# Attention's weighted sum of the values for two token tiles in one run of products of 256 moving columns, and a new order of the first phase

## The chip, the cores and the metric

The kernel runs on one core of a Trainium2 chip. Its engines work side by side and wait for each other by semaphores: PE (TensorE, matrix products; PEld is its weight load), DVE (VectorE), ACT (ScalarE), POOL (GpSimd), and SP, whose queue issues all the DMAs of this kernel. Matrix products write to PSUM banks; ACT and DVE move the results from there to the on-chip memory, SBUF. The metric is the device time of one execution in microseconds (us).

## The reference

Three layers follow each other on 4608 tokens (8 batches of 576), in float32.

```python
# attention: keys and values are averaged over 8 neighbours, so 72 of each per batch and head
k_p = k.reshape(B, H, Sp, pool, D).mean(axis=3); v_p = v.reshape(B, H, Sp, pool, D).mean(axis=3)
scores = scale * np.matmul(q, k_p.transpose(0, 1, 3, 2))            # 8 heads of 64
attn = softmax(scores); x = np.matmul(attn, v_p)                    # 4608 x 512 when heads are joined
# first layer, w_in 512 x 1024, w_out 1024 x 512
h = x @ w_in; solu = h * softmax(h); ln = (solu - mean) / sqrt(var + 1e-6) * g_ln; y = ln @ w_out
# second layer, w_in 512 x 2048, w_out 2048 x 512
h = y @ w2_in; out = (h * sigmoid(1.702 * h)) @ w2_out
```

## The kernel before

Products of float32 numbers are made of three products of float16 halves: an operand is written as a high half and a low half, and high x high, high x low and low x high are summed in PSUM (`PASSES`).

The work has two phases. The first (up to about 515 us) does attention and the first layer for 36 tiles of 128 tokens and prepares the weights of both layers; it writes y to DRAM. The second does the second layer in 6 blocks of 768 tokens, in a written order (`Up`, `Down`), with products of 384 columns. The change does not touch the second phase.

In the first phase each tile t goes through these steps, named as the profile names them:

- `attention(t)`: DMA `qt`; PE writes the scores to the bank `psx`; DVE takes the row maximum `mx`; the exponential `e` is done by ACT in one instruction after a subtraction on DVE, or by ACT in eight instructions, one for each head (`e<-psx,mx`), whichever queue is shorter by the planner's count; then the sum `rs`, its reciprocal, the division (`e<-e,rs`, mostly on POOL), and the weights as float16 in `st`: high half by ACT (`st<-e`), low half by POOL. A DMA transpose writes `st` to `aT` (16 blocks of 128 x 128). PE then multiplies `aT` with the values `vst`: 16 products with 64 weight columns and 128 moving columns, into the one PSUM bank `psv`. Heads 2p and 2p+1 go to partitions 0 to 63 and 64 to 127 of that bank, so they use the two halves of PE's columns. ACT (`xT<-psv`) and DVE (`xT<-psv,xT`) take the result out as two halves. A tile that lies in two batches (4, 13, 22 and 31) has 32 products of 64 columns instead.
- `hidden`: PE multiplies `xT` with `w1i` in four steps k of six products of 512 columns into `psh` (two buffers); DVE takes the maximum `hmx`, ACT the exponential `he`, DVE the product `tt`, which is the last to read `psh`.
- `norm` and `project`, for two tiles together: ACT and POOL write `zs`, a DMA transpose makes `zT`, and PE multiplies it with `w1o` into `psy` (products of 256 columns, `psy<-zT,w1o`).

Tiles 0 to 3 (`ALONE`) are transposed each by itself; from tile 4 on, the transposes of an even tile wait for those of the odd one and are issued together. `aT` and `xT` have two buffers of one tile each. The bank `psv` has one buffer, and also serves the products `psv<-diag,ones`, which spread a maximum (`v_all`, `w2all`) over all partitions. Beside the tiles run the preparation of keys and values (`half`, `kp`, `vp`, `kbd`, `vx`), of `w_in` and `w_out` of both layers (`raw`, `sgw`, `w1i`, `w1o`, `w_f`, `hi`, `lo`), and the scales for them (`w1i_up`, `w1o_up`).

The order of all instructions of the first phase is set when the kernel is built. Each job is a strand of operations; `Plan.run` takes again and again the operation with the lowest score: its start by a table of costs, shifted by how early or late the strand is against its due time, plus a random number of up to `size`. `DRAWS` gives size and seed of these random numbers by stretches of planned time. Each engine then executes its instructions strictly in that order, and SP issues its DMAs strictly in that order.

Of the kernel before, what the change touches and what calls it, by code (L numbers as in the profile page):

```python
# [9 lines left out]
F32 = mybir.dt.float32  # L10
F16 = mybir.dt.float16
# [3 lines left out]
AF = mybir.ActivationFunctionType  # L15
ALU = mybir.AluOpType
# [4 lines left out]
P = 128  # L21
B, H, S, D = 8, 8, 576, 64
# [56 lines left out]
DNS = 7  # L79
SG = 4  # L80
LAST = 90000
LATE = 3000
LATE_TURN = 3000
TTS = 4
DRAWS = ((70e3, 600, 13), (200e3, 150, 4), (330e3, 150, 13), (1e9, 150, 1))
V_TOP = 2.0 ** 14

TOP3 = 2.0 ** -29 * (1 - 2.0 ** -23)
# [95 lines left out]
class Plan:  # L184
# [31 lines left out]
    def drop(self, *tiles):  # L216
        for t in tiles:
            del self.ring_of[t.name]
# [78 lines left out]
def moe_kernel(ctx: ExitStack, tc: tile.TileContext, qT, kT, vT, w_in, w_out, g_ln, w2_in, w2_out, eye, outT):  # L297
# [138 lines left out]
    with ExitStack() as ph:  # L436
# [25 lines left out]
        def there(*ins):  # L462

            return Op(("none",), lambda engine: None, [], ins, {"none": 0})
# [46 lines left out]
        def V(name, *args, **kw):  # L511
            return op(("dve",), name, args, kw)
# [7 lines left out]
        def A(**kw):  # L520
            return op(("act",), "activation", (), kw)

        def D(dst, src=None, turn=False, short=1):
            pairs = dst if src is None else [(dst, src)]

            def emit(engine):
                for pair in pairs:
                    (nc.sync.dma_start_transpose if turn else nc.sync.dma_start)(*pair)

            outs, ins = ([p[i] for p in pairs] for i in range(2))  # L530
            n = sum(math.prod(x.shape) * mybir.dt.size(x.dtype) for x in outs)
            return Op(("sp",), emit, outs, ins, {"sp": n / 360 * (1.23 if turn else short)}, turn)
# [228 lines left out]
        def spans(t):  # L761

            b0, s0 = divmod(t * P, S)
            n = min(P, S - s0)
            parts = [(0, n, b0)]
            if n < P:
                parts.append((n, P - n, b0 + 1))
            return parts
# [88 lines left out]
        def attention(t):  # L857

            yield lambda: t == 0 or q_loaded[t - 1]
            qt = yield New(sb, [P, NPAIR, P], F32, "qt", bufs=2)  # L860
            q_loaded[t] = True
            yield D(qt, qT[t])
            if t < 2:
                tiles[t].due = max(due(t) + LAG_ATT, DUE_ATT + STEP_ATT * t)
            yield lambda: all(k_ready[b] for _, _, b in spans(t)) and (t == 0 or scored[t - 1])
            e = yield New(sb, [P, H, SP], F32, "e", bufs=2)
            yield there(qt, *(kbd[b % 2] for _, _, b in spans(t)))
            ps = yield New(psx, [P, 2, 512], F32, "psx", "psx")
            yield T(
                [  # L870
                    (
                        ps[o : o + n, p // 2, (p % 2) * 2 * SP : (p % 2 + 1) * 2 * SP],
                        qt[:, p, o : o + n],
                        kbd[b % 2][:, p, :],
                        True,
                        True,
                    )
                    for p in range(NPAIR)
                    for o, n, b in spans(t)
                ]  # L880
            )
            scored[t] = True
            drop(qt)
            s4 = ps[:, :, : 4 * SP].rearrange("p a (h k) -> p a h k", k=SP)
            mx = s1("mx", H)
            m3 = mx.rearrange("p (a h) -> p a h", a=2)
            yield V("tensor_reduce", out=m3, in_=s4, axis=AX.X, op=ALU.max, negate=True)
            if plan.free["act"] + ACT_SPARE < plan.free["dve"]:
                for h in range(H):
                    yield A(out=e[:, h], in_=s4[:, h // 4, h % 4], func=AF.Exp, bias=mx[:, h : h + 1])  # L890
                drop(ps)
            else:
                yield V(
                    "tensor_tensor", out=e.rearrange("p (a h) k -> p a h k", a=2), in0=s4,
                    in1=m3.unsqueeze(3).to_broadcast([P, 2, 4, SP]), op=ALU.add,
                )
                drop(ps)
                yield A(out=e, in_=e, func=AF.Exp)
            rs = s1("rs", H)
            yield V("tensor_reduce", out=rs, in_=e, axis=AX.X, op=ALU.add)  # L900
            yield A(out=rs, in_=rs, func=AF.Copy, scale=1.0 / A_TOP, bias=1e-9 / A_TOP)
            yield V("reciprocal", rs, rs)
            yield VG("tensor_tensor", out=e, in0=e, in1=rs.unsqueeze(2).to_broadcast([P, H, SP]), op=ALU.mult)
            yield lambda: t < 2 or turned[t - 2]
            s = st[t % 2]
            yield A(
                out=s[:, :, 0 : 3 * SP].rearrange("p h (r k) -> p h r k", r=3)[:, :, 0:3:2],
                in_=e.unsqueeze(2).to_broadcast([P, H, 2, SP]), func=AF.Copy,
            )
            yield VG("tensor_tensor", out=s[:, :, SP : 2 * SP], in0=e, in1=s[:, :, 0:SP], op=ALU.subtract)  # L910
            drop(e)
            aT = yield New(sb, [P, 2 * H, P], F16, "aT", bufs=2)
            mine = (aT, s.rearrange("p h c -> p (h c)"))
            if t < ALONE:
                yield D(*mine, turn=True)
                turned[t] = True
            elif t % 2:
                yield lambda: to_turn[t - 1] is not None
                yield D([to_turn[t - 1], mine], turn=True)
                turned[t - 1] = turned[t] = True  # L920
            else:
                to_turn[t] = mine
                yield lambda: turned[t]
            yield lambda: all(v_ready[b] for _, _, b in spans(t)) and (t == 0 or valued[t - 1])
            yield there(aT, *(vst[b % 2] for _, _, b in spans(t)))
            ps = yield New(psv, [P, DM], F32, "psv", "psv")
            yield T(
                [
                    (
                        ps[h % 2 * D64 : (h % 2 + 1) * D64, h // 2 * P + o : h // 2 * P + o + n],  # L930
                        vst[b % 2][:, h // 2 * 2 + c, h % 2 * D64 : (h % 2 + 1) * D64],
                        aT[:, 2 * h + c, o : o + n],
                        c == 0,
                        c == 1,
                    )
                    for p in range(NPAIR)
                    for o, n, b in spans(t)
                    for c in range(2)
                    for h in (2 * p, 2 * p + 1)
                ]  # L940
            )
            valued[t] = True
            drop(aT)
            xT = yield New(sb, [P, 2 * KM, P], F16, "xT", bufs=2)
            turned_x = ps.rearrange("p (k t) -> p k t", t=P)
            yield A(out=xT[:, 0:KM], in_=turned_x, func=AF.Copy, scale=1.0 / A_TOP)
            yield V(
                "scalar_tensor_tensor", out=xT[:, KM:], in0=turned_x, scalar=1.0 / A_TOP, in1=xT[:, 0:KM],
                op0=ALU.mult, op1=ALU.subtract,
            )  # L950
            drop(ps)
            x_turned[t] = xT

        class Pair:

# [6 lines left out]
            def hidden(self, j):  # L962
# [3 lines left out]
                if j == 0:  # L966
                    self.sm, self.mean, self.vs = (s1(n, 2, 4) for n in ("hsm", "mean", "vs"))
                xT = x_turned[t]
                yield there(xT)
                ps = yield New(psh, [P, 2, 512], F32, "psh", "psh", 2)  # L970
                hid[t] = True
                plan.now = due(t)
                for k in range(KM):
                    yield lambda: len(first_done) > 2 * k + 1 and first_done[2 * k].ended and first_done[2 * k + 1].ended
                    yield T(
                        [
                            (
                                ps[:, n, :],
                                xT[:, i * KM + k, :],
                                w1i[w][:, k, n * 512 : (n + 1) * 512],  # L980
                                k == 0 and i == 0 and w == 0,
                                k == KM - 1 and i == 1,
                            )
                            for i, w in PASSES
                            for n in range(2)
                        ]
                    )
                drop(xT)
                yield lambda: all(h_ready[b] for _, _, b in spans(t))
                hp = ps.rearrange("p a c -> p (a c)")  # L990
                s = slice(j, j + 1)
# [278 lines left out]
        k_ready, v_ready, h_ready = ([False] * B for _ in range(3))  # L1270
        q_loaded, scored, turned, valued, hid = ([False] * NTILE for _ in range(5))
        x_turned, to_turn = [None] * NTILE, [None] * NTILE
        first_done, upped = [], set()
        begun = {kind: [0] * B for kind in "kv"}
        yp = tok = None
# [449 lines left out]
```

## Time and profile before

| | us |
|---|---|
| median of 3 runs | 1172.25 (1171.01 to 1172.92) |
| the profiled execution | 1171.01 |
| its span, first to last instruction | 1169.0 |
| PE busy in the span | 1125.7 (96%) |
| ACT busy | 754.7 (65%) |
| DVE busy | 724.4 (62%) |
| POOL busy | 617.7 (53%) |

Busy time of PE counts every moment in which a product is under way, also where it waits for its weights; so a stretch of PE at 9 tenths is not one in which nothing can be won. The view by stretches tells where engines are idle, the view of the waits tells for whom, and the view of instructions in order of time tells when.

### The profile page before, as it was taken

To read this page: it belongs to the slowest core of one execution; us is meant where nothing else is said; L and a number is where in the kernel's file an instruction comes from. 1 tells how busy PE (TensorE), PEld (TensorE's weight loads), DVE (VectorE), ACT (ScalarE), POOL (GpSimd) and SP (SyncE) were. 2 spreads that over 40 slices of the span, in tenths; PEclk is the share of its full clock that TensorE was granted. 3 is DMA by queue.
4 is the path that set the end of the run, shared out by engine and by line. 5 is a ranking of instruction groups with operands and counts; after the bars stand their busy time and mean duration, and the time that the engine had idled before them with its cause. 6 is when DMAs were issued, how large, how long until landed. Compare 5 with 4: busy or idle time off the path is not lost.

```text
span 1169.0 us, 19696 instructions
## 1 busy us (share of the span) xinstructions
PE 1125.7 (96%) x7737; PEld 726.1 (62%) x7737; DVE 724.4 (62%) x1105; ACT 754.7 (65%) x997; POOL 617.7 (53%) x643
## 2 busy tenths in 40 slices
PE   4888999999999999999999999999999999999998
PEld 4555676667676667765566656666666665566655
DVE  7988888777677753426753773567266636753650
ACT  6889998989798874737624752674367337625740
POOL 4566999989999985315503530561056016403530
PEclk9989999999999999999999999999999999999999
DMA  9979999999999768355465355536453653463131
GB/s 356 277 191 278 243 280 282 278 275 273 270 244 226 178 172 262 85 195 193 146 200 174 125 176 163 180 127 202 142 174 126 214 178 127 149 202 117 60 121 60
DMA packets 247356, 225.75 MB, mean 193 GB/s; under 512 B 165728, under 2 KB 218080, under 8 KB 246752
## 3 DMA queue, kind: packets, MB, share of 16 engines
q1 hardware_dynamic: 247264, 224.50, 67.0%
q8 instruction: 60, 0.98, 0.3%
q14 instruction: 32, 0.26, 0.1%
HBM read 151.06 MB, written 33.55 MB: 158 GB/s over the span
## 4 chain that ended last, share of the span: by engine, by line
PE 69%; POOL 13%; ACT 6%; DVE 5%; DMA 5%; issue 2%; SPq 1%; POOLq 0%; ACTq 0%; DVEq 0%
PE bank_a L1385 31%; PE bank_d L1385 16%; PE bank_b L1385 8%; PE psy L537 6%; PE psh L537 5%; POOL w_f L496 3%; PE psv L537 2%; POOL lo L496 2%; POOL zs L496 2%; POOL st L496 1%; POOL e L496 1%; PE psx L537 1%; DMA w2i_dram<-lo 1%; POOL q L496 1%; DMA raw<-w_out 1%
## 5 line engine op out<-in xcount | busy, mean ns | idle before, releaser
L1385 PEld LDWEIGHTS <-w2o 128*128 128x128 f16 x2016 | 197.0, 98 | 130.4
L1385 PEld LDWEIGHTS <-w2i 128*128 128x128 f16 x1974 | 193.1, 98 | 129.9 <-issue 2.4
L349 POOL TENSOR_TENSOR w_g<-w_g 128x384 f32<-128x384 f32 x42 | 46.1, 1097 | 399.2 <-ACT w_g L1464 399.2
L1479 DVE SCALAR_TENSOR_TENSOR g<-w_g,gu_b,g 128x1152 f16<-128x1152 f32 (+1 forms) x96 | 175.4, 1828 | 92.0 <-ACT g L1474 91.7
L1385 PE MATMUL bank_a<-ys,w2i 128*128 128x384 f16 x1128 | 205.6, 326 | 0.9 <-ACT c L1404 0.9
L537 PE MATMUL psh<-w1i,xT 128*128 128x512 f16 x864 | 201.8, 384 | 3.5 <-ACT xT L496 3.1
L1385 PE MATMUL bank_a<-g,w2o 128*128 128x384 f16 x1152 | 201.6, 326 | 0.0
L537 PEld LDWEIGHTS <-w1o 128*128 128x128 f16 x1728 | 168.0, 98 | 30.8 <-DMA zT<-zs 2.8
L537 PE MATMUL psy<-zT,w1o 128*128 128x256 f16 x1536 | 176.2, 273 | 3.5 <-DMA zT<-zs 2.3
L1474 ACT ACTIVATE g<-w_g,gu_b 128x1152 f16<-128x1152 f32 (+1 forms) x96 | 134.3, 1411 | 50.3 <-POOL w_g L352 39.3
L1404 ACT ACTIVATE c<-bank_a 128x384 f32<-128x384 f32 x188 | 90.7, 483 | 102.4 <-PE bank_a L1385 101.8
L537 PEld LDWEIGHTS <-xT 128*128 128x128 f16 x864 | 83.4, 99 | 96.3 <-issue 6.0
L1385 PE MATMUL bank_d<-g,w2o 128*128 128x384 f16 x576 | 104.2, 326 | 0.0
L496 POOL TENSOR_TENSOR zs<-tt,zs 128x1024 f16<-128x1024 f32 x36 | 78.4, 2178 | 44.2 <-ACT zs L496 43.8
L1385 PE MATMUL bank_d<-ys,w2i 128*128 128x384 f16 x564 | 101.1, 326 | 0.0
L1464 ACT ACTIVATE w_g<-c,ch_b 128x1536 f32<-128x1536 f32 x47 | 73.8, 1570 | 28.7 <-DVE c L1407 28.7
L352 POOL TENSOR_TENSOR w_g<-w_g 128x384 f32<-128x384 f32 x42 | 83.2, 1982 | 0.0
L1407 DVE SCALAR_TENSOR_TENSOR c<-bank_d,c 128x384 f32<-128x384 f32 x94 | 51.9, 552 | 41.9 <-ACT c L1404 29.6
L496 POOL TENSOR_TENSOR lo<-w_f,hi 128x512 f16<-128x512 f32 (+1 forms) x48 | 65.8, 1389 | 6.6 <-ACT e L496 2.9
L496 DVE TENSOR_REDUCE hmx<-psh 128x1 f32<-128x1024 f32 x36 | 43.8, 1218 | 36.2 <-PE psh L537 36.2
L537 PE MATMUL psx<-kbd,qt 128*128 128x144 f32 (+1 forms) x320 | 47.8, 312 | 15.1 <-ACT kbd L496 9.6
L496 DVE CUSTOM_DVE_ANT_0 tt<-psh,he 128x1024 f32<-128x1024 f32 x36 | 43.8, 1218 | 23.1 <-ACT he L496 22.9
(205 smaller groups left out, 1606.8 us busy)
## 6 DMA issues: line engine op xcount, KB each, us to landing
w2i<-w2i_dram SPq DMA_DIRECT2D x48, 896.0 KB, 4.6
w2o<-w2o_dram SPq DMA_DIRECT2D x84, 512.0 KB, 3.7
half<-kT SPq DMA_DIRECT2D x16, 576.0 KB, 6.4
half<-vT SPq DMA_DIRECT2D x16, 576.0 KB, 6.2
qt<-qT SPq DMA_DIRECT2D x36, 256.0 KB, 4.7
y_dram<-y SPq DMA_DIRECT2D x36, 256.0 KB, 3.5
y<-y_dram SPq DMA_DIRECT2D x48, 192.0 KB, 4.0
raw<-w_in SPq DMA_DIRECT2D x16, 512.0 KB, 7.7
```

The source lines that it names most:

```text
L349: eng.tensor_tensor(out=w[:, 1], in0=q[:, Q12], in1=q[:, Q11], op=ALU.subtract)
L352: eng.tensor_tensor(out=w[:, 3], in0=q[:, Q21], in1=w[:, 2], op=ALU.subtract)
L496: getattr(eng, name)(*args, **kw)
L537: nc.tensor.matmul(*p[:3], start=p[3], stop=p[4], skip_group_check=len(p) > 5)
L1385: nc.tensor.matmul(bank, self.weight(p, kk, w), self.data(p, kk, i), start=(first and kk == 0 and w == 0 and i == 0), stop=(last and kk == ...
L1404: nc.scalar.activation(out=self.c[:, i], in_=getattr(self, bank), func=AF.Copy, scale=self.scale)
L1407: nc.vector.scalar_tensor_tensor(out=self.c[:, i], in0=getattr(self, bank), scalar=self.scale, in1=self.c[:, i], op0=ALU.mult, op1=ALU.add,)
L1464: nc.scalar.activation(out=self.w[:, 0:4], in_=self.c, func=AF.Gelu_apprx_sigmoid, scale=self.ch)
L1474: nc.scalar.activation(out=self.g[s.start][:, 0], in_=self.w[:, s], func=AF.Copy, scale=self.gu)
L1479: nc.vector.scalar_tensor_tensor(out=self.g[s.start][:, 1], in0=self.w[:, s], scalar=self.gu, in1=self.g[s.start][:, 0], op0=ALU.mult, op1 ...
```

## The change

`attention` of an even tile from 4 on ends after its weights are made, and leaves its transpose to the odd tile. A new function `weigh` does the products for one tile (tiles 0 to 3) or for a pair. For a pair `aT` holds both tiles side by side (256 columns), and the products run in two rounds, each with half of the heads: 8 products of 256 columns into `psv`, then out by ACT and DVE, then the other round into the same bank. Where the pair lies in two batches, each weight block has two products whose columns add up to 256. `aT` and `xT` are twice as wide and keep two buffers, so they hold four tiles in place of two. A `hidden` product may begin when two of its four k steps are there (`KM_FIRST`).

```diff
-DRAWS = ((70e3, 600, 13), (200e3, 150, 4), (330e3, 150, 13), (1e9, 150, 1))
+DRAWS = ((70000.0, 600, 12), (80000.0, 150, 12), (200000.0, 150, 118705), (450000.0, 150, 372612), (1000000000.0, 150, 263081))
...
-            aT = yield New(sb, [P, 2 * H, P], F16, "aT", bufs=2)
-            mine = (aT, s.rearrange("p h c -> p (h c)"))
+            if t < ALONE or t % 2 == 0:
+                aT = yield New(sb, [P, 2 * H, 2, P], F16, "aT", bufs=2)
+                mine = (aT[:, :, 0], s.rearrange("p h c -> p (h c)"))
...
+                yield D([other, (aT[:, :, 1], s.rearrange("p h c -> p (h c)"))], turn=True)
...
+            yield from weigh([t] if t < ALONE else [t - 1, t], aT)
+        def weigh(ts, aT):
...
+            wide, rounds = len(ts) * P, len(ts)
+            kr = KM // rounds
+            yield lambda: all(v_ready[b] for _, _, b in parts) and (ts[0] == 0 or valued[ts[0] - 1])
+            yield there(aT, *(vst[b % 2] for _, _, b in parts))
+            xT = yield New(sb, [P, 2, KM, 2 * P], F16, "xT", bufs=2)
+            flat = aT.rearrange("p c j t -> p c (j t)")
+            for r in range(rounds):
+                ps = yield New(psv, [P, DM], F32, "psv", "psv")
+                yield T(
...
+                            flat[:, 2 * h + c, o : o + n],
...
+                yield A(out=xT[:, 0, ks, :wide], in_=turned_x, func=AF.Copy, scale=1.0 / A_TOP)
...
+                drop(ps)
```

The new order shows at three places. The first is ACT at the start, from the first keys (`kbd`) on; `sgw` and `raw` are conversions of `w_in`, `e` and `st` belong to tile 0. Before:

```order
L496 ACTIVATE kbd_133<-kp 64x4x72 x2
L496 ACTIVATE sgw<-raw_z 128x1024
L496 ACTIVATE raw_z<-raw_z 128x1024 x2
L496 ACTIVATE e<-e 128x576
L496 ACTIVATE sgw<-raw_z 128x1024
L496 ACTIVATE raw_z<-raw_z 128x1024 x2
L496 ACTIVATE rs<-rs 128x8
L496 ACTIVATE diag_253<-eye_t,vam 128x128
L496 ACTIVATE st_135<-e 128x8x2x72
```

And now, the last twelve of the twenty rows from `kbd` on that stand ahead of the first `st`:

```order
L497 ACTIVATE raw_z<-raw_z 128x1024
L497 ACTIVATE e<-psx,mx 128x72 x2
L497 ACTIVATE sgw<-raw 128x1024
L497 ACTIVATE e<-psx,mx 128x72 x2
L497 ACTIVATE raw<-raw 128x1024
L497 ACTIVATE e<-psx,mx 128x72
L497 ACTIVATE vx<-vp,v_up 128x4x144
L497 ACTIVATE e<-psx,mx 128x72
L497 ACTIVATE raw<-raw 128x1024
L497 ACTIVATE rs<-rs 128x8
L497 ACTIVATE sgw<-raw 128x1024
L497 ACTIVATE raw<-raw 128x1024
```

Tile 0's exponential is now in eight instructions, and three more `raw`, two more `sgw` and `vx` stand ahead of the first `st`.

The second place is DVE between the conversions of `w_out` and the second tile's `tt` (`ISA tt`). Before:

```order
L496 SCALAR_TENSOR_TENSOR raw<-raw 128x1024
L496 TENSOR_TENSOR e<-psx,mx 128x576
L496 SCALAR_TENSOR_TENSOR xT<-psv,xT 128x512
L496 TENSOR_SCALAR nm<-hmx,h_sc 128x1
L496 SCALAR_TENSOR_TENSOR raw<-raw 128x1024
L496 TENSOR_REDUCE hmx<-psh 128x1
L496 TENSOR_REDUCE rs<-e 128x8
L496 TENSOR_REDUCE mx<-psx 128x8
L496 RECIPROCAL rs<-rs 128x8
L496 TENSOR_SCALAR nm<-hmx,h_sc 128x1
L496 TENSOR_TENSOR e<-psx,mx 128x576
L496 ISA tt,mean<-psh,he 128x1024
```

And now, with the second tile's own `hmx` at the top:

```order
L497 TENSOR_REDUCE hmx<-psh 128x1
L497 TENSOR_SCALAR galln<-galln 128x1
L497 TENSOR_SCALAR nm<-hmx,h_sc 128x1
L497 TENSOR_SCALAR pw_g<-galln 128x1
L497 RECIPROCAL rc_g<-pw_g 128x1
L497 TENSOR_REDUCE mx<-psx 128x8
L497 TENSOR_SCALAR g_up<-rc_g 128x1
L497 TENSOR_SCALAR g_dn<-pw_g 128x1
L497 TENSOR_TENSOR e<-psx,mx 128x576
L497 SCALAR_TENSOR_TENSOR xT<-psv,xT 128x4x128
L497 TENSOR_SCALAR g_col<-g_col,g_up 128x8
L497 ISA tt,mean<-psh,he 128x1024
```

The third tile's `hmx` and the conversions `raw` of `w_out` no longer stand between the second tile's `hmx` and its `tt`.

The third place is PE between the two rounds of the second pair (tiles 6 and 7). Before, between the last product of tile 6 and the first of tile 7:

```order
L537 LDWEIGHTS vst_132
L537 MATMUL psv<-aT,vst_132 64x128
L537 MATMUL psx<-kbd_133,qt 128x144 x4
L537 LDWEIGHTS vst_132
L537 MATMUL psv<-aT,vst_132 64x128
```

And now, between the two rounds of that pair:

```order
L538 LDWEIGHTS vst_132
L538 MATMUL psv<-aT,vst_132 64x256
L538 MATMUL psx<-kbd_133,qt 128x144 x4
L538 LDWEIGHTS vst_132
L538 MATMUL psv<-aT,vst_132 64x256
```

The same four score products stand between the two uses of the bank. Over the whole first phase PE has 416 products of `aT` in place of 640.

## Rows read from the trace of the kernel before

**Rows 1.** Busy time by stretches: stretch, PE, PEld, DVE, ACT, POOL, clock, DMA, GB/s.
```profile
0.00:87.00 87.00, 60.56 (x405) 44.40 (x406) 73.26 (x139) 68.06 (x96) 46.83 (x55) 0.94 0.93 274
117.00:515.00 398.00, 388.52 (x3143) 274.70 (x3142) 263.32 (x475) 316.83 (x459) 326.27 (x391) 1.00 0.92 230
```

**Rows 2.** Instructions in order of time on PE: start, length, columns, idle before.
```profile
431.26 2.78 PE L537 MATMUL psy<-zT,w1o 128*128 128x256 f16 x24
433.88 4.05 PE L537 MATMUL psh<-w1i,xT 128*128 128x512 f16 x18
437.86 0.64 PE L537 MATMUL psv<-aT,vst 128*64 128x128 f16 x16
438.43 2.79 PE L537 MATMUL psy<-zT,w1o 128*128 128x256 f16 x24
...
84.47 0.69 PE L537 MATMUL psv<-aT,vst 128*64 128x64 f16 x32
85.09 1.25 PE L537 MATMUL psx<-kbd,qt 128*128 128x144 f32 x8
```

**Rows 3.** PE's waits: for whom, us in total, times, longest.
```profile
PE psv L537 <- DVE xT L496: 4.6, 6, 1.7
PE psv L537 <- DVE w2all L496: 2.2, 1, 2.2
```

**Rows 4.** Instructions of the tile psv: count, least, median and longest ns.
```profile
L496 ACT ACTIVATE xT<-psv x36: 571/586/618, 35.4 to 453.7; 128x512 f16<-128x512 f32 x36
L496 DVE SCALAR_TENSOR_TENSOR xT<-psv,xT x36: 678/689/693, 36.7 to 454.8; 128x512 f16<-128x512 f32 x36
```

**Rows 5.** PE in order of time around the second tile's end.
```profile
69.07 0.22 PE L537 MATMUL psy<-diag,ones 128*128 128x128 bf16 x1 [2.41 <-ACT kp L496]
71.40 0.27 PE L537 MATMUL psy<-diag,ones 128*128 128x128 bf16 x1 [2.11 <-DVE mean L496]
71.46 2.77 PE L537 MATMUL psh<-w1i,xT 128*128 128x512 f16 x6
74.02 2.13 PE L537 MATMUL psx<-kbd,qt 128*128 128x144 f32 x8
```

**Rows 6.** Busy time by stretches, the same place.
```profile
70.40:77.20 6.80, 5.80 (x18) 3.44 (x18) 4.47 (x23) 4.04 (x8) 5.40 (x13) 0.50 0.87 174
74.00:76.00 2.00, 2.00 (x10) 1.89 (x9) 0.00 (x0) 0.69 (x2) 1.92 (x4) 0.50 0.75 81
```

**Rows 7.** DVE and ACT in order of time, the same place.
```profile
60.22 1.21 DVE L496 TENSOR_REDUCE hmx<-psh 128x1 f32<-128x1024 f32 x1
69.92 1.22 DVE L496 CUSTOM_DVE_ANT_0 tt<-psh,he 128x1024 f32<-128x1024 f32 x1
...
67.91 0.21 ACT L496 ACTIVATION_READ_ACCUMULATOR he<-psh,nm,h_sc 128x1 f32 x1
```

**Rows 8.** ACT in order of time, and the tile e: the start of the kernel.
```profile
12.21 2.13 ACT L496 ACTIVATE raw_z<-raw_z 128x1024 uint32<-128x1024 uint32 x2
20.28 1.17 ACT L496 ACTIVATE st<-e 128x1152 f16<-128x1152 f32 x1 [1.17 <-POOL e L496]
...
L496 ACT ACTIVATE e<-e x35: 666/672/705, 14.2 to 414.1; 128x576 f32<-128x576 f32 x35
L496 ACT ACTIVATE e<-psx,mx x8: 303/330/366, 381.0 to 394.2; 128x72 f32<-128x72 f32 x8
```

**Rows 9.** PE in order of time: the first weighted sum and the first hidden product.
```profile
31.12 0.64 PE L537 MATMUL psv<-aT,vst 128*64 128x128 f16 x16 [0.66 <-DMA vst<-vx]
36.06 2.59 PE L537 MATMUL psh<-w1i,xT 128*128 128x512 f16 x6 [3.12 <-ACT xT L496]
```

**Rows 10.** DMA issues (count, median us to landing), and a wait of SP's queue.
```profile
aT<-st SPq DMA_TRANSPOSE x36, 5.0
zT<-zs SPq DMA_TRANSPOSE x36, 4.0
...
SPq L528 <- PE psv L537: 10.2, 5, 4.7
```

More of the change, by code (lines that the diff above doesn't have):

```diff
@@ L81 @@
 LAST = 90000
+KM_FIRST = 2
 LATE = 3000
@@ L918, in attention @@
                 yield lambda: to_turn[t - 1] is not None
-                yield D([to_turn[t - 1], mine], turn=True)
+                aT, other = to_turn[t - 1]
+                yield D([other, (aT[:, :, 1], s.rearrange("p h c -> p (h c)"))], turn=True)
                 turned[t - 1] = turned[t] = True
             else:
[L922 to L952, printed above, removed]
+                to_turn[t] = aT, mine
@@ new lines, in attention @@
+                return
+            yield from weigh([t] if t < ALONE else [t - 1, t], aT)
+        def weigh(ts, aT):
+            parts = []
+            for j, t in enumerate(ts):
+                for o, n, b in spans(t):
+                    if parts and parts[-1][2] == b:
+                        parts[-1][1] += n
+                    else:
+                        parts.append([j * P + o, n, b])
+            wide, rounds = len(ts) * P, len(ts)
[7 more added lines that the diff above has]
+                yield T(
+                    [
+                        (
+                            ps[h % 2 * D64 : (h % 2 + 1) * D64, (h // 2 - r * kr) * wide + o : (h // 2 - r * kr) * wide + o + n],
+                            vst[b % 2][:, h // 2 * 2 + c, h % 2 * D64 : (h % 2 + 1) * D64],
+                            flat[:, 2 * h + c, o : o + n],
+                            c == 0,
+                            c == 1,
+                        )
+                        for p in range(r * kr, (r + 1) * kr)
+                        for o, n, b in parts
+                        for c in range(2)
+                        for h in (2 * p, 2 * p + 1)
+                    ]
+                )
+                if r == rounds - 1:
+                    for t in ts:
+                        valued[t] = True
+                    drop(aT)
+                ks = slice(r * kr, (r + 1) * kr)
+                turned_x = ps.rearrange("p (k t) -> p k t", t=wide)
+                yield A(out=xT[:, 0, ks, :wide], in_=turned_x, func=AF.Copy, scale=1.0 / A_TOP)
+                yield V(
+                    "scalar_tensor_tensor", out=xT[:, 1, ks, :wide], in0=turned_x, scalar=1.0 / A_TOP,
+                    in1=xT[:, 0, ks, :wide], op0=ALU.mult, op1=ALU.subtract,
+                )
+                drop(ps)
+                for t in ts:
+                    x_parts[t] += kr
+                    x_turned[t] = xT
+            x_left[xT.name] = len(ts)
@@ L968, in hidden @@
                 xT = x_turned[t]
-                yield there(xT)
+                mine = slice(0 if t < ALONE else t % 2 * P, P if t < ALONE else (t % 2 + 1) * P)
+                yield lambda: x_parts[t] >= KM_FIRST or x_parts[t] == KM
+                yield there(xT[:, :, : x_parts[t], mine])
                 ps = yield New(psh, [P, 2, 512], F32, "psh", "psh", 2)
@@ L973, in hidden @@
                 for k in range(KM):
+                    yield lambda: x_parts[t] > k
                     yield lambda: len(first_done) > 2 * k + 1 and first_done[2 * k].ended and first_done[2 * k + 1].ended
@@ L978, in hidden @@
                                 ps[:, n, :],
-                                xT[:, i * KM + k, :],
+                                xT[:, i, k, mine],
                                 w1i[w][:, k, n * 512 : (n + 1) * 512],
@@ L987, in hidden @@
                     )
-                drop(xT)
+                yield lambda: xT.name in x_left
+                x_left[xT.name] -= 1
+                if not x_left[xT.name]:
+                    drop(xT)
                 yield lambda: all(h_ready[b] for _, _, b in spans(t))
@@ L1272, in moe_kernel @@
         x_turned, to_turn = [None] * NTILE, [None] * NTILE
+        x_parts, x_left = [0] * NTILE, {}
         first_done, upped = [], set()
```

## The prediction

> **What bounds the kernel now.** I read the busy time by stretches first. From 117 to 515 us, the bulk of the first phase, PE is busy 388.5 of 398 us, and no other engine over 326 [rows 1]; in the first 87 us it is busy 60.6 of 87, with DVE (73.3) and ACT (68.1) both busier than PE. So the first phase has two regimes: a start in which DVE and ACT set the pace, and a long part in which PE does. Second I read PE in order of time, to see what a weighted sum costs there: 16 products of 128 columns start at 437.86 and the next work at 438.43, so 0.57 us [rows 2]. Third, PE's waits: the bank `psv` is waited for in most of those after the start, 4.6 us in six waits for the eviction of an earlier tile and 2.2 us in one for a maximum [rows 3]. Last, the costliest single place on PE, around 70 us, from three views: two waits of 2.41 and 2.11 us, then products at half speed [rows 5, 6]. The second phase is untouched, and begins when the first ends.
>
> All sums are made against the profiled execution: 1171.01 us, of which 1169.0 are the span and 2.0 lie around it. The median shown is 1172.25, 1.24 more; I add the sum to the median, as another kernel's median would carry the same surplus.
>
> **The product itself: 0.** Before, a pair of tiles has two groups of 16 products, 2 x 0.57 = 1.14 us on PE. What are the 0.57? A product of 256 columns on the whole array takes 2.62 / 24 = 0.109 us (431.26 to 433.88), so 128 columns take 0.055; 16 of them one after another would be 0.87. Only 0.57 pass, so the two heads of a pair run side by side, in 8 x 0.055 = 0.44 us, and 0.13 us are entry and exit. Now a pair of tiles has two rounds of 8 products of 256 columns: 4 side-by-side pairs x 0.109 = 0.44, plus entry and exit 0.13: again 0.57 a round. The number of columns and of groups is the same; what goes is half of the weight loads, and these lie beside the products. Bounds: if entry and exit vanished, 32 rounds x 0.13 = 4.2 us are won. If wide products did not run side by side, a round is 8 x 0.109 + 0.13 = 1.0, and 32 x 0.43 = 13.8 us are lost; nothing but the width speaks for that. I take 0, since the 64-column form fits too: 32 products in 0.62 us [rows 2] is shorter than 16 x 0.055, so pairs overlap at either width. The pairs with two batches change as little: tile 4 and tile 5 cost 0.62 + 0.57, and now two rounds of eight narrow and eight 192-column products.
>
> The Trainium skill has a rule that would give more: TensorE: Matmul & The Clock Gate, section "Back-to-back issue gap", says that in a stream of weight loads and products the spacing is set by both, some 81 ns at 128 columns and 131 ns at 512. By it halving the loads would pay; but here 16 loads and products of 128 columns pass in 0.57 us, 36 ns each, so the trace does not show loads that set the pace.
>
> **Evictions: 0.** ACT and DVE still take 512 columns out of `psv` 36 times, at 0.59 and 0.69 us [rows 4]: 32 for pairs, 4 for the first tiles.
>
> **The bank psv: +0.4.** Both rounds use the one bank, so the second waits until ACT and DVE have emptied it, about 1.3 us plus the way between the engines, and more when their queues hold other work. In PE's order I counted how often at most 2.6 us of PE work (by the rates of rows 2) stand between one use of the bank and a following weighted sum: 18 times before, 19 times now. Of these, follow-ups of one weighted sum on another are 8 before and 12 now; sums behind a maximum are 10 and 7. The waits seen are 6.8 us over 18 places, 0.38 each, so +0.4. Bounds: all gone, -6.8; each of the four added short follow-ups at the longest wait seen, 1.7: +6.8.
>
> **The early stall: -4.** At 66.7 to 71.5 PE stands for 2.41 + 2.11 us, and then runs at half clock until 77.2 (0.50 granted, the 1.2 GHz level): six products of 512 columns take 2.56 us from 71.46 to 74.02, where 18 took 3.98 at 433.88, so 1.33 for six. That is 1.2 lost, and as much again in the next 3 us: 6.9 in all. The next hidden product could not start before, since both `psh` buffers were full until the second tile's `tt` ended at 71.1; and `tt` came 8.5 us after its own `hmx` had ended, behind the third tile's `hmx` and two conversions, though ACT's `he` had ended at 68.1 [rows 7]. In the new order DVE has only small scalings, one `mx`, one subtraction and one `xT` between the two, so `tt` waits for `he`, and `psh` comes free some 2 to 4 us earlier. PE's order helps too: 30 products of `psh` now stand before the product for `w1o` that waited. But the whole 6.9 cannot be won: DVE is the busier engine here, and idle for only about 2.3 us of it, 74.0 to 76.0 in full [rows 6]. I take 4, between 2.3 (DVE's idle time) and 6.9; if the stall forms anew elsewhere, 0.
>
> **The start: +1.** Tile 0's exponential is now eight instructions on ACT, 8 x 0.33 = 2.6 us in place of one of 0.67, and three `raw` and two `sgw` (1.07 each, [rows 8]) and `vx` (an estimate of 0.6, half of an `st` for half of its columns) go first: 2.0 + 5.3 + 0.6 = 7.9 us, less 1.2 in which ACT was idle. So the first `st` ends some 6 us later than 21.45, and the first weighted sum, at 31.12 before, comes at about 37, the first hidden product at 38 to 39 in place of 36.06 [rows 9]. Behind a late `st` there is nothing on ACT that was not going to be done: the conversions that overtake it are the ones the hidden product needs for its weights. So PE gets most of it back when the four steps of that product run without a break. Bounds: -1 (they are ready together) to +6 (all of it stays).
>
> **The wider buffers: 0.** SP's queue waited five times for a weighted sum to free `aT`, 10.2 us in all [rows 10]; with four tiles of room that goes. No wait of PE for `aT` is in the view of the waits, so nothing shows on PE. Bound: the bank's 4.6 us, if evictions came earlier through it.
>
> A rule of the Trainium skill speaks against the change here. DMA: Bandwidth & Descriptors, section "Latency and other measured facts", says that a DMA transpose whose middle dimension is not contiguous moves some 30% less. The target of `aT` becomes that (blocks of one tile lie 256 columns apart). But `zT` has that form already, with the same size, and lands in 4.0 us at the median against 5.0 for today's `aT` [rows 10]; the trace does not agree, and the sum takes nothing for it.
>
> **Sum.** 0 + 0.4 - 4 + 1 + 0 = -2.6 us, and -1 more for the half clock behind the one long bank wait (2.2 us, [rows 3]) if, as likely as not, that meeting does not recur: half of 2.2. So -3.6: 1167.4 against the profiled execution, 1168.7 for the median.
>
> **Rivals.**
> - More is won: the early stall goes in full (-6.9), and so do most bank waits (-4 of 6.8), since tiles are finished further ahead in wider buffers. For it: these are all waits on work that was only queued late. Against: ACT and DVE are at 80% and 66% even in PE's part, so queues stay. 1172.25 - 10.9, about 1161.5.
> - It does not do what it says: the stall of 70 us is DVE's pace, not its order, and moves to the next place. DVE is busy 73.3 of the first 87 us, the work is the same, and every other term is near nothing: 1172.
> - Slower: the late first tile decides. DVE sits in its queue behind tile 0's sum `rs`, which needs all eight exponentials; what follows it there (the last maxima of `w_in`, and so the scale of `w1i`) is late too, and a regime paced by DVE never gets it back. It decides if more than the 4 us of the early stall stay: +6 from the start, 0 from the stall less a bank wait or two, about +4: 1176.
> - Wide products do not run side by side, or transposes to the split target are slow enough to be waited for: +13.8 for the first, 1186.
>
> **How the numbers follow.** Forecast (1166 to 1171) 0.36; more is won 0.21; no change 0.22; slower from the start 0.16; wide products or transposes 0.05. The likeliest is 1168.7. A measurement of this kernel tells 0.2%, 2.3 us, from no change. Faster by more than that: 0.34 of the forecast's and all of the second, 0.55. Slower: 0.16 + 0.05 = 0.21. Within: the rest, 0.24. The range that holds 8 in 10 reaches from 1160.5 (a part of the second beyond it) to 1175.5 (half of the slower case inside).
>
> **What would show it.** In the new profile a round of eight wide products should be followed by PE's next work after 0.55 to 0.60 us; under 0.5, or at 1.0, that step is wrong. The first weighted sum should stand near 37 us and the first hidden product near 39. Around 65 to 77 us there should be no two waits of over 2 us in a row and no half clock; if there are, elsewhere before 117 us, the second rival holds. Waits for `psv` should sum to 6 to 8 us. The stretch from 515 us on, shifted, should be the same. What would make the prediction wrong above all is a start whose delay is passed on by DVE, or an order whose queues meet better than I can see from counts.

## The result, and the profile after

The changed kernel takes 1184.69 us (median of 6, 1180.32 to 1188.49), the kernel before 1172.65 beside it. The ratio is 1.0095, 95% interval 1.0077 to 1.0113: slower, where I had said 1168.7 and faster. The profiled execution took 1188.49 us, its span 1186.7; before it was 1171.01 and 1169.0. From span to span 17.7 us are lost, between the medians 12.0: the profiled execution is the slowest of the changed kernel's six, that of the kernel before the fastest of its six, so some 6 of the 17.7 us belong to these two executions and not to the change. PE's busy time grew by 3.9 (1125.7 to 1129.6), its idle time by 13.8 (43.3 to 57.1).

Where? Busy time of the changed kernel by stretches, columns as in [rows 1]:

```profile
0.00:87.00 87.00, 56.72 (x389) 42.09 (x390) 70.69 (x135) 68.06 (x103) 47.98 (x54) 0.97 0.84 267
117.00:200.00 83.00, 74.74 (x555) 50.72 (x553) 64.78 (x111) 67.36 (x98) 69.52 (x78) 0.94 1.11 256
117.00:531.00 414.00, 394.24 (x2942) 273.93 (x2940) 271.18 (x482) 315.84 (x457) 318.88 (x387) 0.98 0.91 222
```

and of the kernel before, the stretch that [rows 1] does not show apart:

```profile
117.00:200.00 83.00, 81.30 (x665) 57.21 (x664) 68.39 (x117) 73.63 (x107) 79.69 (x91) 1.00 1.05 270
```

The first phase now ends near 531 us, not 515. Between 117 us and its end PE is idle for 19.8 us (414 less 394.2) where it was for 9.5. From 117 to 200 us every engine does less than before (PE 74.74 for 81.30, GpSimd 69.52 for 79.69), and PE's clock is 0.94 of full in place of 1.00.

PE's waits in the changed kernel, as [rows 3]:

```profile
PE psv L538 <- DVE xT L497: 13.4, 5, 5.5
PE psv L538 <- DMA aT<-st: 9.2, 6, 3.4
PE psv L538 <- DVE w2all L497: 1.2, 1, 1.2
```

The eviction of an earlier weighted sum is waited for 13.4 us, before 4.6. The wait of a weighted sum for its transposes, 9.2 us, had no line before. The longest of both from 60 to 200 us, on PE in order of time:

```profile
89.17 1.06 PE L538 MATMUL psv<-aT,vst 128*64 128x64 f16 x16 [5.50 <-DVE xT L497]
...
125.26 0.30 PE L538 MATMUL psv<-aT,vst 128*64 128x128 f16 x4 [2.57 <-DMA aT<-st]
127.14 0.85 PE L538 MATMUL psv<-aT,vst 128*64 128x128 f16 x12 [1.57 <-DMA aT<-st]
...
168.57 1.07 PE L538 MATMUL psv<-aT,vst 128*64 128x192 f16 x16 [3.44 <-DMA aT<-st]
```

Around each the granted clock is at the 1.2 GHz level, here at the second and the third:

```profile
126.80:130.20 3.40, 3.06 (x18) 1.51 (x18) 1.05 (x2) 2.17 (x3) 3.40 (x3) 0.50 1.01 315
167.80:174.60 6.80, 6.03 (x28) 2.60 (x28) 2.96 (x5) 2.49 (x4) 6.80 (x7) 0.50 0.86 259
```

In the first phase of this execution 30.6 us are spent at that clock, before 13.6, which is more than enough for the 3.9 us of added busy time: six products of `psh` are listed with 2.59 us at 127.92, at half clock, and with 1.46 at 121.23. In large part it is the execution's own: its mean granted clock is 0.987 of full, some 31 us at half clock, and that of the other five 0.990 to 0.992, 19 to 24 us.

What I had promised of the product itself is there. One round of eight wide products, on PE:

```profile
153.80 0.63 PE L538 MATMUL psv<-aT,vst 128*64 128x256 f16 x8
154.35 1.25 PE L538 MATMUL psx<-kbd,qt 128*128 128x144 f32 x8
```

0.55 us to the next work, against 0.57 for the group of 16 in [rows 2].

### The profile page after: what moved, and what is told of

Its sections match the earlier page's. It is cut to its first block, busy times and chain, and to the rows that moved or that the text cites. A ratio compares the mean times of both kernels' runs of the same rounds, so it can differ in the third digit from the quotient of the medians.

```text
span 1186.7 us, 19252 instructions
## 1 busy us (share of the span) xinstructions
PE 1129.6 (95%) x7513; PEld 724.3 (61%) x7513; DVE 731.4 (62%) x1108; ACT 753.9 (64%) x1004; POOL 611.2 (52%) x639
## 4 chain that ended last, share of the span: by engine, by line
PE 69%; POOL 10%; ACT 6%; DMA 5%; DVE 5%; issue 3%; SPq 1%; POOLq 0%; ACTq 0%; DVEq 0%
PE bank_a L1416 31%; PE bank_d L1416 15%; PE bank_b L1416 8%; PE psy L538 7%; PE psh L538 6%; PE psv L538 3%; POOL lo L497 2%; POOL w_f L497 2%; POOL e L497 1%; POOL st L497 1%; DVE raw L497 1%; DMA w2i_dram<-lo 1%; DMA aT<-st 1%; DMA raw<-w_in 1%; PE psx L538 1%
## 5 line engine op out<-in xcount | busy, mean ns | idle before, releaser
L497 POOL TENSOR_TENSOR lo<-w_f,hi 128x512 f16<-128x512 f32 (+1 forms) x44 | 60.7, 1393 | 6.4 <-ACT hi L497 2.7
L538 PE MATMUL psx<-kbd,qt 128*128 128x144 f32 (+1 forms) x320 | 44.6, 299 | 18.7 <-DMA qt<-qT 10.8
L538 PEld LDWEIGHTS psx<-kbd,qt 128*128 128x128 f32 (+1 forms) x320 | 40.0, 186 | 29.5 <-issue 15.4
```

Source lines behind the costliest of these rows:

```text
L497: getattr(eng, name)(*args, **kw)
L538: nc.tensor.matmul(*p[:3], start=p[3], stop=p[4], skip_group_check=len(p) > 5)
```

## The experiments

Theory O: the pairing is worth next to nothing, and the new order of the first phase costs. Theory P: the pairing itself costs, since a pair needs both transposes before it can begin, and uses the one bank twice in a row.

### Other draws for both structures

Only the table of random numbers is changed: the kernel before with the table of the changed one, and the reverse; then both without random numbers.

```diff
-DRAWS = ((70e3, 600, 13), (200e3, 150, 4), (330e3, 150, 13), (1e9, 150, 1))
+DRAWS = ((70000.0, 600, 12), (80000.0, 150, 12), (200000.0, 150, 118705), ...)   # e1, on before
+DRAWS = ((1e9, 0, 1),)                                                           # e3, on before
```

The second and fourth run make the like edits of the changed kernel.

> The kernel before, unchanged but for its random numbers: it gets the sizes and seeds that the changed kernel has. Theory O (the loss comes from the order that happens to be drawn, not from pairing): this one is slower than before too, by some 5 to 18 us (1177 to 1190). Theory P (pairing itself costs, since a pair's product needs both transposes and the one bank twice): about as before, 1169 to 1176.

> The changed kernel with the random numbers of the kernel before. Theory O: a draw like any other, anywhere from 1173 to 1195, on no side of the changed kernel's 1184.7 for a reason. Theory P: 1182 to 1190.

> The kernel before with random numbers of size zero: the planner's own order. Theory O: slower than before by 5 to 20 us. Theory P: within 4 us of before.

> The changed kernel with random numbers of size zero. Theory O: within 6 us of e3_before_no_draws on either side. Theory P: some 12 us above it.

Measured: 1187.15 (ratio 1.0126, 1.0109 to 1.0143), 1190.98 (1.0161, 1.0145 to 1.0178), 1184.40 (1.0096, 1.0071 to 1.0121) and 1180.72 (1.0071, 1.0052 to 1.0090). Every other order is slower than the kernel before, also with the products of one tile. Without random numbers the pair's kernel has the lower median of the two, though the intervals overlap. The kernel before with the other table has the changed kernel's waits, though it pairs nothing:

```profile
PE psv L537 <- DVE xT L496: 13.1, 6, 5.8
PE psv L537 <- DMA aT<-st: 7.9, 3, 3.4
```

That is for O, but not clean: a table does not give the same order to two structures.

### The orders exchanged

So I wrote the orders down, operation by operation, and let each structure run in the other's. A pair's first half stands where the even tile's product and eviction stood, its second half where the odd one's stood; nothing else moves. One line has to move for it, so that the second buffer of `xT` is not asked for before the first is free:

```diff
-            xT = yield New(sb, [P, 2, KM, 2 * P], F16, "xT", bufs=2)
             for r in range(rounds):
                 ps = yield New(psv, [P, DM], F32, "psv", "psv")
                 yield T(...)
+                if r == 0:
+                    xT = yield New(sb, [P, 2, KM, 2 * P], F16, "xT", bufs=2)
```

The reverse run takes the functions of the kernel before, with `aT` and `xT` at `bufs=4`, and the changed kernel's order.

> The changed kernel's pairs, but every engine works in the order of the kernel before: the product of a pair's first half stands where the even tile's product stood, that of its second half where the odd tile's stood, and the evictions likewise (xT is allotted behind the first product, so that nothing else is moved). Theory O (the order is what costs): within 0.3% of the before of this call, about 1170 to 1176 us, and the longest waits of the changed kernel (5.5 us for an eviction at 89 us, 3 to 4 us for transposes at 125 and 168 us) are gone. Theory P (the pairing itself costs): about 1183 us or more, since both transposes and the bank still have to come first.

> The reverse: the kernel before's products, one tile at a time and 128 columns wide, each evicted by itself, but every engine works in the order of the changed kernel (the even tile's product stands where the pair's first half stood; aT and xT get four buffers of a tile each, the same memory as two of a pair). Theory O: as slow as the changed kernel, 1181 to 1188 us, with PE's waits for aT of 5 to 10 us in all at the same places (125 to 127 and 168 us) and the eviction's wait at 89 us. Theory P: near the before of this call, about 1173 us.

Measured: pairs in the old order 1168.87 (1167.96 to 1170.46; ratio 0.9963, 0.9950 to 0.9977), a little below what theory O said; single tiles in the new order 1183.64 (1180.31 to 1186.05; 1.0087, 1.0070 to 1.0103). The time goes with the order and not with the pairing. Nor is it the half clock: the single tiles' profiled execution was granted 0.997 of the full clock, some 7 us at half clock, and took 1184.30 us. PE's waits, first of the pairs in the old order, where no line names `aT`:

```profile
PE psv L636 <- DVE xT L595: 5.9, 9, 1.7
```

then of the single tiles in the new order:

```profile
PE psv L639 <- DVE xT L598: 11.8, 5, 5.8
PE psv L639 <- DMA aT<-st: 7.1, 3, 2.6
```

Why the old order does not wait shows on SP's queue (a line is the time in which it issues) beside PE's. Pairs in the old order:

```profile
108.58 6.96 SPq L627 DMA_TRANSPOSE zT<-zs  x2
115.63 3.90 SPq L627 DMA_TRANSPOSE aT<-st  x2
...
132.42 0.64 PE L636 MATMUL psv<-aT,vst 128*64 128x128 f16 x16
```

The changed kernel:

```profile
111.57 9.52 SPq L529 DMA_TRANSPOSE zT<-zs  x2
121.18 3.77 SPq L529 DMA_TRANSPOSE aT<-st  x2
...
121.23 1.46 PE L538 MATMUL psh<-w1i,xT 128*128 128x512 f16 x6
```

In the old order the transposes of tiles 8 and 9 have been issued at 119.5 and their weighted sum starts at 132.42, with 12.9 us of room. In the new order they have been issued at 124.95, and PE, which came to the product at 122.69, starts it at 125.26 and stops in it again until 127.14. PE comes to the product 9.7 us sooner than in the old order, and SP to the end of the transposes 5.4 us later.

Pairs in the old order are faster than both kernels. That 0.37% (0.23 to 0.50) is the worth there of the pairing with its wider buffers, 4.3 us. One profile of each does not show where it lies: the spans are 1168.7 and 1169.0, though the medians are 4 apart.

### One more draw

> The kernel before, products of one tile, with the same four stretches and sizes of the draw but the seeds 100 to 103 in place of 13, 4, 13 and 1. Theory O: a drawn order of the kernel before is worth about as much as any other, 1178 to 1192 us, so that 1173 us is the lucky end. Theory P: within 0.4% of the kernel before.

1192.47 (1.0165, 1.0146 to 1.0184). This is just above theory O's range. With the two above, three other orders of the kernel before cost 11 to 19 us; how the table of its own order was chosen, no run shows. PE from 117 to 200 us in this one:

```profile
117.00:200.00 83.00, 72.58 (x543) 49.47 (x542) 60.08 (x120) 66.86 (x97) 66.24 (x79) 0.96 1.06 262
```

A slow order need not wait for the transposes: PE waits 1.6 us for `aT` here, and in the kernel before without random numbers 1.5:

```profile
PE psv L537 <- DMA aT<-st: 1.5, 1, 1.5
```

### Can the waits be moved away?

Three places of the changed kernel's order, by hand; all else stays. The list names operations of the order and is not code.

```diff
 ACT:  w1o, w1o, w1o, w1o,
-      w1o, w1o, zs, w1o, w1o, tt, xT (tiles 4 and 5, first half), st, zs, e, xT (second half)
+      xT (first half), w1o, w1o, zs, w1o, xT (second half), w1o, tt, st, zs, e
 PE:
-      psv (tiles 8 and 9, first half), psh, psx (tile 12), psv (second half), psh, psh, psh, psx (tile 13), psy
+      psh, psx (tile 12), psh, psh, psv (first half), psh, psx (tile 13), psy, psv (second half)
       (tiles 12 and 13 likewise behind three pieces of psh)
```

> The changed kernel in its own order but for three places. Tiles 4 and 5: the first half's eviction on ACT goes ahead of four w1o conversions, and the second half's product ahead of the psx of tile 8. Tiles 8 and 9: the first half's product goes behind three more pieces of psh, the second half's behind them. Tiles 12 and 13: the first half's goes behind three pieces of psh, the second behind a piece of psy and of psh. Theory O: the waits of 5.5, 4.1 and 3.4 us go, and with them up to three stretches at half clock (1.7 us lost in each 3.4 us of it), so 8 to 18 us less than the changed kernel: 1167 to 1177 us. Theory P: the transposes are late for what follows too, and less than 5 us comes back: 1180 us or more.

1187.36 (1.0116, 1.0099 to 1.0133): nothing came back, where theory O, for which the exchange had spoken, had 1167 to 1177. By stretches, this kernel:

```profile
60.00:90.00 30.00, 26.80 (x194) 17.34 (x193) 25.41 (x56) 25.91 (x39) 17.04 (x20) 1.00 0.57 155
90.00:117.00 27.00, 19.68 (x134) 12.72 (x133) 22.96 (x46) 24.04 (x38) 18.03 (x28) 1.00 1.11 268
```

and the changed kernel:

```profile
60.00:90.00 30.00, 22.95 (x174) 15.81 (x172) 25.46 (x55) 25.97 (x39) 17.23 (x20) 0.93 0.60 169
90.00:117.00 27.00, 26.56 (x170) 16.34 (x167) 24.75 (x55) 25.64 (x42) 18.91 (x31) 0.95 1.11 265
```

PE wins 3.9 us up to 90 us and loses 6.9 up to 117. ACT and DVE do the same work in the first stretch as they did (25.9 and 25.4 of 30), so PE only came sooner to what they had not yet made. The operations tell the same: the hidden products behind tiles 4 and 5 start at 85.81 us in place of 90.17, the products of `w1o` behind them at 117.86 in place of 115.99. At the second place PE waited for a load instead:

```profile
131.27 2.26 PE L636 MATMUL psx<-kbd,qt 128*128 128x144 f32 x8 [5.42 <-DMA qt<-qT]
```

That `qt` stood in SP's queue behind the same transposes. So a second try leaves the place of tiles 4 and 5 alone, and puts the loads of `qt` for tiles 12 and 13 ahead of the transposes:

```diff
-SP: zT (pair 1) x2, aT (tiles 8 and 9) x2, y_dram, qt (12), qt (13)
+SP: qt (12), zT (pair 1) x2, qt (13), aT (tiles 8 and 9) x2, y_dram
```

> The changed kernel in its own order but for two places: the products of tiles 8 and 9 and of tiles 12 and 13 moved behind later pieces of psh, as in the run with three places, and SP's load of qt for tile 12 put ahead of the zT transposes, that for tile 13 ahead of the aT transposes, so that the psx of tile 12 does not wait for it (5.42 us there). The eviction of tiles 4 and 5 stays where the changed kernel has it. If single waits of PE are the price of this order (local), 4.1 and 3.4 us of waits and some 5 us of half clock go: 1171 to 1177 us. If the engines that feed PE are late there as well (given back), PE waits at the next place instead and the time stays at 1181 to 1188 us.

1180.74 (1178.99 to 1185.88; 1.0080, 1.0054 to 1.0105), some 4 us under the changed kernel, but the intervals overlap. From 117 to 200 us:

```profile
117.00:200.00 83.00, 74.74 (x575) 51.08 (x573) 66.06 (x118) 71.08 (x105) 73.04 (x81) 1.00 1.09 267
```

PE is busy for 74.74 us, as in the changed kernel, but the clock is back at 1.00 and it gets further: the product of a maximum that the changed kernel starts at 188.04 starts 5.3 us sooner (this profiled execution is the fastest of its six). First the changed kernel, then this one:

```profile
188.04 0.22 PE L538 MATMUL psv<-diag,ones 128*128 128x128 bf16 x1
182.76 0.22 PE L636 MATMUL psv<-diag,ones 128*128 128x128 bf16 x1
```

The waits for `aT` fell from 9.2 to 3.1, and others stand in their place:

```profile
139.30 2.75 PE L636 MATMUL psh<-w1i,xT 128*128 128x512 f16 x12 [1.54 <-DVE mean L595]
143.45 0.22 PE L636 MATMUL psv<-diag,ones 128*128 128x128 bf16 x1 [1.40 <-ACT diag L595]
...
176.23 5.40 PE L636 MATMUL psy<-zT,w1o 128*128 128x256 f16 x48 [1.77 <-ACT y L595]
```

Single waits as the whole price would have won 8 to 14 us (1171 to 1177); the medians lie 4 apart, and 1180.74 is 0.3 below the range for an outcome in which all is given back. So a few microseconds may be local, and the larger part is given back at the next places.

### Is one feeding engine short?

Two edits of both kernels, each in its own order. The first narrows the low parts of `w2` on GpSimd and stores the high ones in their place; the second leaves the stores of the low parts out.

```diff
-yield VG("tensor_tensor", out=lo[:, s], in0=w[:, s], in1=hi[:, s], op=ALU.subtract)
+yield VG("tensor_tensor", out=lo[:, s, :32], in0=w[:, s, :32], in1=hi[:, s, :32], op=ALU.subtract)   # e9, e10
...
-yield D(self.dst[1], lo)
+yield D(self.dst[1], hi)                       # e9, e10
+(no store; the second phase reads hi twice)    # e11, e12
```

> The changed kernel in its own order, with less work for GpSimd: the subtraction that makes the low parts of w2 (lo<-w_f,hi, 48 of them, 1.16 us and 2.6 us each) covers 32 of 256 columns, and the high part is stored a second time in place of the low part, so the low parts of w2 are wrong and the bytes moved are the same. Some 55 us of GpSimd's work between 127 and 440 us go. Theory G (the new order starves GpSimd, which before worked 79.7 of the 83 us from 117 to 200): most of the 11.5 us comes back, and the distance to the same edit of the kernel before is under 5 us. Theory D (the DMA queue binds there) and theory N (the orders of the queues hold each other up, no one engine is short): the distance stays at 9 to 14 us.

> The same edit of the kernel before in its own order: low parts of w2 narrowed to 32 columns and the high part stored in their place. All theories: 1166 to 1173 us, as PE is busy for 81.3 of the 83 us from 117 to 200 and for 96 to 97 of each 100 behind them; it is the control that e9 is measured against.

> The changed kernel in its own order, with less for the DMA queue: the 16 stores of the low parts of w2 (448 KB each, 7.2 MB in all, between 153 and 450 us) are left out, and the second phase reads the high parts twice, so the low parts are wrong. At 260 GB/s that is some 27 us of transfers. Theory D (the DMA queue binds the new order: 1.11 of its share from 117 to 200 us against 1.05 before): most of the 11.5 us comes back, to 1172 to 1178 us, and the distance to the same edit of the kernel before is under 5 us. Theories G and N: the distance stays at 9 to 14 us.

> The same edit of the kernel before in its own order: the stores of the low parts of w2 left out, the high parts read twice. All theories: 1166 to 1173 us; the control for e11.

With less for GpSimd: 1177.06 (ratio 1.0047, 1.0027 to 1.0066) in the new order and 1167.15 (0.9955, 0.9942 to 0.9969) in the old, 9.9 us apart, where it was 12.0 without the edit; theory N had 9 to 14. With less for the DMA queue: 1185.07 (1.0105, 1.0074 to 1.0136) and 1167.52 (0.9959, 0.9944 to 0.9973), 17.6 apart, more than any theory said. So neither GpSimd nor the amount of data explains the 12.0: less work for GpSimd wins about as much in the old order, and taking 7.2 MB of stores from the new one won nothing that can be measured. ACT and DVE were not relieved in this way; from 117 to 200 us both do less than in the old order, which speaks against them and does not test them. Theory N is left, that the queues hold each other up, and it is left by exclusion and not shown; which first meeting of queues in the new order starts it stays open.

## Why the prediction was wrong

The step that failed is to read the price of a new order off the waits of the old one. The sum priced the new order at three places where it met such a wait, and put it at nothing from 117 us on for the one reason that the old order hardly waits there. The runs show that the order is the price: 1183.64 us for single tiles in the new order and 1168.87 for pairs in the old, with 1173.12 for the kernel before beside both. Of the 13.8 us that PE is idle more, 10.3 come after 117 us. What in the new order starts it stays open.

That pairs in the old order came out next to my 1168.7 is luck. The early stall, from which I took 4 us, is still there:

```profile
PE psy L636 <- ACT kp L595: 5.3, 2, 2.9
PE psy L636 <- DVE mean L595: 2.1, 1, 2.1
```

Term by term:

- **The product, 0: right.** 0.55 us a round against the forecast 0.55 to 0.60. Single tiles in the new order, with 16 products of 128 columns, are as slow as pairs there (1183.64 and 1184.69).
- **Evictions, 0: right.** 36 at 593 ns on ACT and 691 on DVE, as in [rows 4].
- **The bank, +0.4: wrong for this order.** I forecast 6 to 8 us of waits at `psv` and there are 24.5 in all, 13.4 of them for an eviction. For the pairing itself the term is near: in the old order all waits at `psv` come to 9.5 us with pairs and 8.5 with single tiles, while single tiles in the new order wait 11.8 for evictions alone. I had counted PE work between two uses of the bank. The longest wait, 5.50 us at 89.17, came because ACT was busy with conversions of `w1o` when the bank was full, which PE's order does not tell:

```profile
80.13 4.02 ACT L497 ACTIVATE w1o<-raw,w1o_gs 128x512 f16<-128x512 f32 x6
84.05 1.06 ACT L497 ACTIVATE zs<-tt 128x1024 f16<-128x1024 f32 x1
84.99 1.40 ACT L497 ACTIVATE w1o<-raw,w1o_gs 128x512 f16<-128x512 f32 x2
86.27 1.25 ACT L497 ACTIVATE tt<-tt,mean,a 128x1024 f32<-128x1024 f32 x1
87.40 0.60 ACT L497 ACTIVATE xT<-psv 128x512 f16<-128x512 f32 x1
```

- **The early stall, -4: right at its place.** The two waits of [rows 5] are 0.44 and 0.96 us now, and the clock is 1.00 from 66 to 78 us:

```profile
76.22 0.22 PE L538 MATMUL psy<-diag,ones 128*128 128x128 bf16 x1 [0.44 <-ACT kp L497]
77.40 4.19 PE L538 MATMUL psy<-half,eye_t 128*128 128x144 f32 x32 [0.96 <-DVE w1o_all L497]
```

  The 5.50 us at 89.17, with 6.8 us at half clock around it, took it back. The rival of a stall that moves to the next place described this one, though ACT held it and not DVE, as the rival had it.
- **The start, +1: mis-sized.** The first `st` ended 5.1 us later (26.53 for 21.45; I had said some 6, where 7.9 less 1.2 are 6.7). The first weighted sum came at 34.18, earlier than the 37 I forecast; but the first hidden product came at 44.54 and not at 39, behind a second weighted sum that waited for the bank:

```profile
34.18 0.64 PE L538 MATMUL psv<-aT,vst 128*64 128x128 f16 x16 [0.91 <-DMA aT<-st]
...
41.47 1.06 PE L538 MATMUL psv<-aT,vst 128*64 128x128 f16 x16 [3.51 <-DVE xT L497]
...
44.54 4.23 PE L538 MATMUL psh<-w1i,xT 128*128 128x512 f16 x18
```

  PE is busy for 34.6 of the first 60 us, before for 38.8: 4.2 us, near the bound of +6. So the slower rival was right on the size of this part, and it does not account for the rest: from 60 to 117 us PE is busy for 49.5, before for 48.8, and three quarters of the added idle time come later.
- **Wider buffers, 0: where that step is written down.** "No wait of PE for `aT` is in the view of the waits, so nothing shows on PE." The view was of the old order, in which the transposes of tiles 8 and 9 have 12.9 us of room. The new order had used that up, and PE waits 9.2 us for `aT`. The bound I gave this step (4.6 won) had no loss in it. The width is not the cause: single tiles in the new order wait 7.1 us for `aT`, and the kernel before with the other table, its buffers unchanged, 7.9. Nor are these waits the whole price, since other slow orders have 1.5 and 1.6 us of them.
- **Transposes to a split target, 0: right.** `aT` lands in 5.0 us at the median, as in [rows 10], and `zT` in 4.5 for 4.0:

```profile
aT<-st SPq DMA_TRANSPOSE x36, 5.0
zT<-zs SPq DMA_TRANSPOSE x36, 4.5
```

- **Half clock, -1: wrong in sign.** 17.0 us more are spent at it in the first phase of the profiled execution, and in the other five some 5 to 10 more than the 14 of the kernel before, by their mean clocks (that one was granted 0.994).

## What to carry to other kernels

When a change draws the order of a long phase anew, its price is the order's, and the waits listed for the old order say nothing of waits that the old order had no cause to make. Take the old order over by hand first and measure the change in that: here it turned +0.95% into -0.37%. And moving one engine's work past a wait may only move the wait: of two tries here one won nothing and the other 4 us of 12.

## What was not expected of the hardware

Two transposes of `zT` held SP's queue for 9.52 us in the new order, for 6.96 with pairs in the old order, and for 8.15 in the kernel before. What stands behind them is issued only then: in the run with three places moved, PE waited 5.42 us for `qt`, a plain load, in that way. Products of 256 columns on half of the array run side by side as those of 128 do: eight pass in 0.55 us, where at 0.109 us each, the rate of 256 columns on the whole array in [rows 2], one after another would take 0.87.
